# Softmax and MLP on one core: value products in halves, row maxima computed in the MLP, one score bank in four copied by VectorE

## The chip, the core and the metric

The kernel runs on one core of a Trainium2 chip. The metric is the device time of one execution in microseconds (us), median of several runs. PE is TensorE, PEld its weight loads, DVE is VectorE, ACT is ScalarE, POOL is GpSimd, and SP is the engine whose queue issues most of the DMAs. PSUM has eight banks of 128 x 512 f32; scores and products land there.

## What is computed

For x of 2048 tokens by 448 channels:

```
g = sigmoid((x * gate_w).sum(-1, keepdims=True))
# attention, 16 heads of 28 channels, one shared key and value head
q = (x @ wq) per head; k = x @ wk; v = x @ wv
p = softmax(q k^T * 28 ** -0.5)
a = (p v) of all heads @ wo
# token mixer and MLP
h  = gelu(layernorm(x) @ w1);  hs = shifted h @ w2;  x1 = x + hs
b  = x1 + gelu(layernorm(x1) @ w3) @ w4          # 448 -> 1792 -> 448
out = g * a + (1 - g) * b
```

Most products are made in three passes of fp32r, from high and low parts of both operands; the value products and the output projection are plain f32.

## The kernel before

All engines follow the order in which the program text issues their instructions; each engine works through its own queue in order, and semaphores join the queues.

**First stage** (to about 100 us): query projections for 16 units, keys, values and gate go to a DRAM tensor qd and come back in other layouts. A unit u = 4b + g is a block b of 512 tokens with a group g of four heads; its queries are a tile of 128 x 512, 32 rows per head, of which 28 hold queries, and two rows (28 and 29) are free for the negative row maximum in a high and a low part. They multiply two rows of ones in the keys, so the scores come out with the maximum already subtracted.

**MLP** (to about 402 us): for each of four blocks b, 14 iterations f of 128 hidden channels. `w3_part` (L614) makes 11 matmuls into one of two banks, ACT takes gelu twice (gh rounded at L625, gf in f32 at L626), DVE subtracts for the low part gl (L627). The second layer follows two iterations later: `w4_part` (L630), three matmuls for each of four token tiles into four accumulation banks. In the last block the function `fill` (L610) slips in the one maximum that unit 0 needs. A maximum is `max_all` (L200): four matmuls of the query tile with 32 keys per head (khd) and a reduction on DVE, then `max_end` (L220): negate, split, transpose on DVE, and eight small DMAs on SP that write the two rows into the unit's query tile qh. The maximum is taken over 32 keys only; sums that come out too large are found at the end, and then a branch, not taken here, computes everything again.

**Attention** (to about 954 us): 16 units of eight steps v, two key tiles of 128 keys each. `q_begin` (L718) splits the queries of a unit into qh and ql, two units ahead, at v=6. In a step:

- `scores` (L795), for each of the two key tiles: three passes, each of four matmuls (one per head, in four row groups), into four banks taken from the front of a list;
- `exps` (L803): ACT exponentiates the four banks into SBUF tiles p and returns each bank to the end of the list. READ is the order, DRAIN (empty) the banks that DVE would copy first, `late_exps` their exponentials;
- at v=2 the maximum of the next unit (`max_all`, `max_end`) and `recip` of the last unit's sums, at v=3 `norm`;
- at v=4 to 7 `wo_job` (L757): the output projection of the last unit, one token tile, into one bank, and `wo_add` (L774), which DVE adds to the output;
- `values` (L817) of the step before: eight f32 matmuls of 512 columns into one bank, and DVE adds it to the tile o (L828; at the first step a copy, L826).

The list holds all eight banks. With f32 operands each matmul is two records in the trace. `sums_begin` (L735) fetches the sums, `recip` (L740) takes their reciprocals and sends them through DRAM to 128 partitions, `norm` (L751) multiplies. A closing part (L870 on) finishes the last unit's tokens.

Of the kernel before, what the change touches and what calls it, by code (L numbers as in the profile page):

```python
# [16 lines left out]
P = 128  # L17
# [19 lines left out]
def f32(ap):  # L37
    return ap.bitcast(F32)
# [3 lines left out]
def gated_mix_kernel(  # L42
# [44 lines left out]
    def misc_tile(name):  # L87
        return psA.tile([P, 512], F32, tag="misc", bufs=1, name=name)
# [86 lines left out]
    def q_load(u, raw):  # L175
        b, g = divmod(u, NG)
        qr_of[u] = raw
        nc.sync.dma_start(raw, qd[g, :, 512 * b:512 * b + 512])
# [13 lines left out]
    NU = NB * NG  # L192
    qr_of, qh_of, ql_of = {}, {}, {}
    mx_of = {}
    mc_of = {}

    def max_tile(name):
        return psA.tile([P, 512], F32, tag="mx", bufs=1, name=name)
# [1 line left out]
    def max_all(u, ps):  # L200
        mx_of[u] = late.tile([P, 4, 4], F32, tag="mr", bufs=1, name=f"mr_{u}")
        for t in range(4):
            nc.tensor.matmul(ps[:, t * P:(t + 1) * P], qh_of[u][:, t * P:(t + 1) * P], khd, start=True, stop=True)
        nc.vector.reduce_max(mx_of[u].rearrange("p j t -> p t j"), ps.rearrange("p (t j k) -> p t j k", t=4, j=4), axis=AX.X)
# [12 lines left out]
                nc.vector.reduce_max(mr[:, j, t:t + 1], mk, axis=AX.X)  # L217
        mx_of[u] = mr

    def max_end(u):  # L220
        mr = mx_of.pop(u).rearrange("p j t -> p (j t)")
        mc = late.tile([P, 32], F32R, tag="mc", bufs=1, name=f"mc_{u}")
        nc.vector.tensor_scalar(mc[:, 0:16], mr, -1.0, None, op0=ALU.mult)
        nc.vector.scalar_tensor_tensor(mc[:, 16:32], mr, -1.0, f32(mc)[:, 0:16],
                                       op0=ALU.mult, op1=ALU.subtract)
        mrow = late.tile([P, 32], F32, tag="mrow", bufs=1, name=f"mrow_{u}")
        nc.vector.transpose(mrow, f32(mc))
        for k in range(2):
            for p in range(4):
                r = 32 * p + 16 * k  # L230
                nc.sync.dma_start(
                    f32(qh_of[u])[DH + k:P:32, :].rearrange("j (t p q) -> p j t q", p=4, q=32)[p], mrow[r:r + 16, :])

    ctx2 = ExitStack()

# [366 lines left out]
    with tc.tile_pool(name="s2", bufs=1, reuse_waits="tile") as s2, \  # L602
# [2 lines left out]
            for n in range(n0, n1):  # L605
                nc.gpsimd.tensor_scalar(x1[:, n, :], x1[:, n, :], gi[:, n:n + 1], None, op0=ALU.mult)

        fills = [lambda: max_all(0, misc_tile("m_0")), lambda: max_end(0)]

        def fill():  # L610
            if fills:
                fills.pop(0)()

        def w3_part(b, f):  # L614
            i, k = divmod(f, 2)
# [23 lines left out]
        for b in range(NB):  # L639
            acc = [ps2.tile([P, 512], F32, tag="acc", bufs=4, name=f"acc_{b}_{t}") for t in range(4)]  # L640
            gs = {}
            for f in range(NF):
                if f == 9 and b + 1 < NB:
                    mv, rs = layernorm_stats(s2a, b + 1)
                if f == 10 and b + 1 < NB:
                    xt4 = big(f"xt4_{b + 1}")[:, 0:4 * D].rearrange("p (f t j) -> p f t j", f=NE, t=4)
                if f in (10, 11) and b + 1 < NB:
                    for t in (2 * f - 20, 2 * f - 19):
                        xn = s2a.tile([P, 512], F32, tag="xn", bufs=1, name=f"xn_{b + 1}_{t}")[:, 0:D]
                        layernorm_norm(b + 1, t, mv, rs, xn, xt4)  # L650
                if f == 11 and b + 1 < NB:
                    xt_write(b + 1, xt4)
                    ln_read(b + 1)
                gs[f] = w3_part(b, f)
                if b == 0 and f % 2 and f < 11:
                    split_w3((f + 3) // 2)
                    split_w4((f + 3) // 2)
                    if f < 9:
                        load_w34((f + 5) // 2, s2a if f == 1 else s2)
                if b == 1 and f == 0:  # L660
                    nc.gpsimd.tensor_tensor(gg, invE, gz, ALU.pow)
                    nc.vector.tensor_scalar(gg, gg, 1.0, None, op0=ALU.add)
                    nc.vector.reciprocal(gg, gg)
                    nc.vector.tensor_scalar(gi, gg, -1.0, 1.0, op0=ALU.mult, op1=ALU.add)
                if b == NB - 1 and f == 4:
                    weigh_x1(0, 4 * b)
                if b == 1 and f in (0, 2, 4, 6):
                    load_k(f // 2, s2a.tile([P, 512], F32, tag="xn", bufs=1, name=f"kf_{f // 2}"))
                if b == 1 and f in (1, 3, 5, 7):
                    split_k(f // 2)  # L670
                if b == 2 and f == 1:
                    nc.gpsimd.memset(f32(khd), 0.0)
                    for j in range(4):
                        nc.sync.dma_start(f32(khd)[32 * j:32 * j + DH, j, :], f32(kH)[0:DH, 0:MK])
                    q_load(0, s2a.tile([P, 512], F32, tag="xn", bufs=1, name="qr_0"))
                if b == 2 and f == 5:
                    q_split(0, qh0, ql0)
                if f >= 2:
                    for t in range(4):
                        w4_part(f - 2, t, gs[f - 2], acc)  # L680
                        if b > 2 and t % 2 == 0 and f < NF - 1:
                            fill()
            for t in range(4):
                w4_part(NF - 2, t, gs[NF - 2], acc, NF - 2 if b == NB - 1 else NF - 1)
                if b + 1 < NB:
                    ln_split(b + 1, t, t + 1)
# [7 lines left out]
        assert not fills  # L694
    ctx2.close()


    with tc.tile_pool(name="s3", bufs=1, reuse_waits="tile") as s3, \
# [7 lines left out]
        def take():  # L706
            return banks.pop(0)
# [107 lines left out]
                nc.scalar.activation(p_of[u, kt][j], p_of[u, kt][j], AF.Exp, scale=SCALE)  # L815

        def values(u, v, add=True):  # L817
            pv = take()
            for kt in (2 * v, 2 * v + 1):
                ps = p_of.pop((u, kt))  # L820
                for j in range(4):
                    nc.tensor.matmul(pv[32 * j:32 * j + 32, :], vext[:, kt, :], ps[j],  # L822
                                     start=(kt % 2 == 0), stop=(kt % 2 == 1), tile_position=(0, 32 * j))
            if v == 0:
                o_of[u] = s3.tile([P, 512], F32, tag="o", bufs=2, name=f"o_{u}")
                nc.vector.tensor_copy(o_of[u], pv)  # L826
            elif add:
                nc.vector.tensor_add(o_of[u], o_of[u], pv)  # L828
            else:
                return pv  # L830
            banks.append(pv)

        READ = (0, 1, 2, 3)
        DRAIN = ()
        WO_AT = (4, 5, 6, 7)
        M_AT = 2

        for k in range(NU * NV):
            u, v = divmod(k, NV)
            if v == 6 and u + 2 < NU:  # L840
                q_begin(u + 2)
                q_fetch(u + 3)
            for kt in (2 * v, 2 * v + 1):
                exps(u, kt, scores(u, kt))
            for kt in (2 * v, 2 * v + 1):
                late_exps(u, kt)
            if v == 2 and sums:
                norms.append(recip(*sums.pop()))
            if v == 3 and norms:
                norm(*norms.pop())  # L850
            if v == M_AT and u + 1 < NU:
                ps = take()
                max_all(u + 1, ps)
                banks.append(ps)
                max_end(u + 1)
            job = None
            if v in WO_AT:
                if u:
                    job = wo_job(u - 1, WO_AT.index(v))
                else:  # L860
# [10 lines left out]
        pv = values(u, NV - 1, False)  # L871
# [4 lines left out]
        tq = [bank(f"oq_{t}")[:, 0:P] for t in range(4)]  # L876
        rr = s3.tile([P, 2, 2, 4], F32, name="rr4")
        on4 = s3.tile([P, 4, P], F32, name="on4")

# [30 lines left out]

        def keep_warm(n):
            for _ in range(n):
                nc.tensor.matmul(banks[0][:, 0:256], warm[:, 0:P], warm, start=True, stop=True)

        for t in range(4):
            nc.vector.tensor_add(o[:, toks[t]], o[:, toks[t]], pv[:, toks[t]])
# [35 lines left out]
        with tc.If(again > 0, label="redo"):  # L952
            for b in range(NB):
                for g in range(NG):
# [1 line left out]
                    q_fetch(u)  # L956
                    q_begin(u)
                    max_full(u, bank)
                    max_end(u)
# [67 lines left out]
```

## Time and profile before

| what | us |
|---|---|
| median of 3 runs | 971.56 (971.14 to 971.71) |
| the profiled execution | 970.74 |
| its span | 968.9 |
| ACT busy in the span | 647.0 |
| DVE busy in the span | 345.7 |

The profile is one execution. A row of a timeline gives the start and the length in us, the engine, the line, the operation, the tiles written and read, and in brackets the idle time of the engine before it with what ended it. A row of a group gives count, busy time, mean length in ns and idle time before. A row of a table by stretches gives, after the stretch and its length, the busy time of PE, PEld, DVE, ACT and POOL with their instruction counts, the granted share of the TensorE clock, the share of the DMA engines and their GB/s. The end of matmuls is modelled, so a PE that looks busy may be waiting.

### The profile page before, as it was taken

The numbers are of one execution on the slowest core, as the hardware profiler recorded it, in microseconds if no ns is written. First come the engines' busy times: TensorE is split into PE (matmuls) and PEld (weight loads), VectorE is DVE, ScalarE is ACT, GpSimd is POOL, SyncE is SP. The second block draws the span as 40 slices with busy tenths as digits, with TensorE's granted clock in tenths as the row PEclk, the third lists the DMA queues.
The fourth block names the chain that finished last, engine by engine and source line by source line (L and its number), as shares of the span: only waits on it lengthen the run. The fifth ranks groups of instructions, "written<-read, shape, count | busy, mean of one in ns | idle before, by whom it ended". The sixth has DMA issues, their size and how long they took to land. (4 is left out here: it accounts for less than half of the span.)

```text
span 968.9 us, 19222 instructions
## 1 busy us (share of the span) xinstructions
PE 960.1 (99%) x7571; PEld 589.3 (61%) x7571; DVE 345.7 (36%) x636; ACT 647.0 (67%) x1262; POOL 74.9 (8%) x105
## 2 busy tenths in 40 slices
PE   9999999999999999999999999999999999999996
PEld 7788888888888888644444444444444444444442
DVE  5663354433413421233333333333233332333323
ACT  5532444422222222589999999999999999999993
POOL 2242200221002400200000000000000000000000
PEclk9999999999999999999999999999999999999999
DMA  9703342300300300100000010000010000100001
GB/s 317 263 27 76 103 162 83 89 22 10 93 1 1 82 1 1 60 13 14 14 23 14 24 50 24 14 13 24 24 51 15 14 25 13 53 23 2 13 13 42
DMA packets 38753, 46.22 MB, mean 48 GB/s; under 512 B 8880, under 2 KB 27008, under 8 KB 38656
## 3 DMA queue, kind: packets, MB, share of 16 engines
q1 hardware_dynamic: 35632, 39.45, 13.6%
q10 hardware_dynamic: 3024, 5.47, 1.6%
q8 instruction: 61, 1.00, 0.4%
q14 instruction: 36, 0.29, 0.1%
HBM read 32.85 MB, written 11.67 MB: 46 GB/s over the span
## 5 line engine op out<-in xcount | busy, mean ns | idle before, releaser
L810 ACT ACTIVATE p<-bank 128x512 f32<-128x512 f32 x1024 | 510.9, 653 | 42.7 <-PE bank L800 42.7
L822 PE MATMUL bank<-p,vext 128*32 128x512 f32 x2048 | 245.9, 598 | 0.0
L800 PEld LDWEIGHTS bank<-qh,kH 30*128 30x128 f32 x1024 | 86.2, 182 | 141.8 <-ACT p L810 128.4
L800 PE MATMUL bank<-qh,kH 30*128 30x512 f32 x1024 | 168.4, 465 | 0.1
L625 ACT ACTIVATE gh<-g 128x512 fp32r<-128x512 f32 x55 | 32.8, 597 | 187.6 <-PE g L134 187.6
L800 PE MATMUL bank<-qh,kL 28*128 28x512 f32 x1024 | 137.9, 404 | 0.0
L822 PEld LDWEIGHTS bank<-p,vext 128*32 128x32 f32 x2048 | 59.9, 110 | 127.3 <-issue 101.1
L800 PE MATMUL bank<-ql,kH 28*128 28x512 f32 x1024 | 131.3, 389 | 0.0
L828 DVE TENSOR_TENSOR o<-o,bank 128x512 f32<-128x512 f32 x111 | 76.3, 687 | 123.9 <-PE bank L822 72.9
L627 DVE TENSOR_TENSOR gl<-gf,gh 128x512 fp32r<-128x512 f32 x55 | 38.3, 696 | 168.0 <-ACT gf L626 168.0
L636 PE MATMUL acc<-w4l,gh 128*128 128x448 f32 x220 | 80.4, 366 | 0.0
L635 PE MATMUL acc<-w4h,gh 128*128 128x448 f32 x220 | 80.4, 365 | 0.0
L637 PE MATMUL acc<-w4h,gl 128*128 128x448 f32 x220 | 80.3, 365 | 0.0
L800 PEld LDWEIGHTS bank<-ql,kH 28*128 28x128 f32 x1024 | 73.6, 185 | 9.6
L131 PE MATMUL g<-al,w3h 128*128 128x512 f32 x168 | 65.7, 391 | 0.0
L130 PE MATMUL g<-ah,w3h 128*128 128x512 f32 x168 | 65.6, 390 | 0.0
L132 PE MATMUL g<-ah,w3l 128*128 128x512 f32 x168 | 65.6, 390 | 0.0
L800 PEld LDWEIGHTS bank<-qh,kL 28*128 28x128 f32 x1024 | 62.1, 184 | 0.0
L763 PE MATMUL bank<-wof,on 128*32 128x448 f32 x512 | 61.2, 551 | 0.0
L775 DVE SCALAR_TENSOR_TENSOR ot<-bank,gg,ot 128x448 f32<-128x448 f32 x44 | 30.1, 684 | 85.7 <-PE bank L763 56.9
L635 PEld LDWEIGHTS acc<-w4h,gh 128*128 128x128 f32 x220 | 41.3, 188 | 4.7
L902 POOL TENSOR_TENSOR ot<-y,ot 128x448 f32<-128x448 f32 x1 | 1.2, 1162 | 553.5 <-ACT y L901 553.5
(188 smaller groups left out, 997.1 us busy)
## 6 DMA issues: line engine op xcount, KB each, us to landing
qd<-qf ACTq DMA_DIRECT2D x16, 256.0 KB
qr<-qd SPq DMA_DIRECT2D x16, 256.0 KB
rb<-rd SPq DMA_DIRECT2D x15, 256.0 KB
x<-in_x_dram SPq DMA_DIRECT2D x4, 896.0 KB
xd<-xt SPq DMA_DIRECT2D x16, 224.0 KB
w34raw<-in_w_dram SPq DMA_DIRECT2D x7, 512.0 KB
out_dram<-ot SPq DMA_DIRECT2D x15, 224.0 KB
w34raw<-in_w_dram SPq DMA_DIRECT2D x7, 448.0 KB
```

Source lines behind the costliest of these rows:

```text
L130: nc.tensor.matmul(ps, wh[:, c, :], ah[:, c, :], start=(c == 0), stop=False)
L131: nc.tensor.matmul(ps, wh[:, c, :], al[:, c, :], start=False, stop=False)
L132: nc.tensor.matmul(ps, wl[:, c, :], ah[:, c, :], start=False, stop=False)
L627: nc.vector.tensor_sub(gl, gf, f32(gh))
L635: nc.tensor.matmul(ps, gh[:, tok], w4h[i][:, k, :], start=(f == 0), stop=False)
L636: nc.tensor.matmul(ps, gh[:, tok], w4l[i][:, k, :], start=False, stop=False)
L637: nc.tensor.matmul(ps, gl[:, tok], w4h[i][:, k, :], start=False, stop=(f == stop))
L763: nc.tensor.matmul(ps[32 * j:32 * j + 32, 0:D], on_of[u][:, tok], wof[:, g, :], start=True, stop=True, tile_position=(0, 32 * j))
L800: nc.tensor.matmul(bs[j], w, a, start=(i == 0), stop=(i == 2), tile_position=(32 * j, 0))
L810: nc.scalar.activation(ps[j], bs[j], AF.Exp, scale=SCALE)
L822: nc.tensor.matmul(pv[32 * j:32 * j + 32, :], vext[:, kt, :], ps[j], start=(kt % 2 == 0), stop=(kt % 2 == 1), tile_position=(0, 32 * j))
L828: nc.vector.tensor_add(o_of[u], o_of[u], pv)
```

## The change

- **Maxima.** All 16 are computed in the MLP, one per iteration: units 0 to 6 in block 2 at f=2 to 8, units 7 to 15 in block 3 at f=0 to 8. For each, SP loads the unit's queries from qd (`max_load`), DVE rounds them into qh0 (`max_cast`, ahead of the iteration's second-layer matmuls on PE and behind gl on DVE), PE and DVE take the maximum behind the second layer, and in the next iteration the two rows go to qd by eight DMAs, four on SP and four on ACT (`max_send`). In the attention the query loads bring the rows along. `max_end` no longer sends; only the branch at the end still asks it to.
- **Values.** Each step's value products are made in two halves of 256 columns, each with a bank of its own, and DVE adds each half by itself.
- **Banks.** READ is (0, 3, 1, 2) and DRAIN is (3,): DVE copies the fourth head's bank to p in SBUF and returns it; ACT exponentiates that copy in place, behind the six other exponentials of the step.
- **Reciprocals.** `recip` moves from v=2 to the end of v=1, `norm` from v=3 ahead of the values to the end of v=3.
- The load of unit 0's queries moves to block 3, f=11, and its split to f=13; the closing part takes another bank for the matmuls that keep PE's clock up.

```diff
-    def max_end(u):
+    def max_end(u, again=False):
...
         nc.vector.transpose(mrow, f32(mc))
+        row_of[u] = mrow
+        if again:
+            max_send(u, f32(qh_of[u]), nc.sync)
+
+    def max_send(u, q, other):
+        mrow = row_of.pop(u)
         for k in range(2):
             for p in range(4):
                 r = 32 * p + 16 * k
-                nc.sync.dma_start(
-                    f32(qh_of[u])[DH + k:P:32, :].rearrange("j (t p q) -> p j t q", p=4, q=32)[p], mrow[r:r + 16, :])
+                (other if k else nc.sync).dma_start(
+                    q[DH + k:P:32, :].rearrange("j (t p q) -> p j t q", p=4, q=32)[p], mrow[r:r + 16, :])
...
-        fills = [lambda: max_all(0, misc_tile("m_0")), lambda: max_end(0)]
...
+        def max_load(u):
+            if u < NU:
+                q_load(u, s2a.tile([P, 512], F32, tag="xn", bufs=1, name=f"qm_{u}"))
+
+        def max_cast(u):
+            qh_of[u] = qh0
+            nc.vector.tensor_copy(qh0, qr_of.pop(u))
+            max_load(u + 1) if u != 6 else None
...
+                    max_load(0)
+                u = f - 2 if b == 2 and 2 <= f <= 8 else f + 7 if b == 3 and f <= 8 else None
+                if b == 2 and f == 12:
+                    max_load(7)
+                if row_of:
+                    w, = row_of
+                    max_send(w, qd[w % NG, :, w // NG * 512:w // NG * 512 + 512], nc.scalar)
+                if u is not None:
+                    max_cast(u)
+                if b == NB - 1 and f == 11:
                     q_load(0, s2a.tile([P, 512], F32, tag="xn", bufs=1, name="qr_0"))
-                if b == 2 and f == 5:
+                if b == NB - 1 and f == 13:
                     q_split(0, qh0, ql0)
                 if f >= 2:
                     for t in range(4):
                         w4_part(f - 2, t, gs[f - 2], acc)
-                        if b > 2 and t % 2 == 0 and f < NF - 1:
-                            fill()
+                if u is not None:
+                    max_all(u, max_tile(f"m_{u}") if u % 2 else misc_tile(f"m_{u}"))
+                    max_end(u)
...
         def values(u, v, add=True):
-            pv = take()
...
+            pvs = []
+            for q in (slice(0, 256), slice(256, 512)):
+                pv = take()
+                for kt in (2 * v, 2 * v + 1):
+                    for j in range(4):
+                        nc.tensor.matmul(pv[32 * j:32 * j + 32, q], vext[:, kt, :], p_of[u, kt][j][:, q],
+                                         start=(kt % 2 == 0), stop=(kt % 2 == 1), tile_position=(0, 32 * j))
+                if v == 0:
+                    nc.vector.tensor_copy(o_of[u][:, q], pv[:, q])
+                elif add:
+                    nc.vector.tensor_add(o_of[u][:, q], o_of[u][:, q], pv[:, q])
+                pvs.append(pv)
+                if add:
+                    banks.append(pv)
+            return pvs
+
+        READ = (0, 3, 1, 2)
+        DRAIN = (3,)
...
-            if v == 2 and sums:
-                norms.append(recip(*sums.pop()))
-            if v == 3 and norms:
-                norm(*norms.pop())
-            if v == M_AT and u + 1 < NU:
-                ps = take()
-                max_all(u + 1, ps)
-                banks.append(ps)
-                max_end(u + 1)
...
                 values(*divmod(k - 1, NV))
-                if v == 0:
-                    sums.append(sums_begin(u - 1, o_of[u - 1]))
+            if u and v == 0:
+                sums.append(sums_begin(u - 1, o_of[u - 1]))
+            if u and v == 1:
+                norms.append(recip(*sums.pop()))
+            if u and v == 3:
+                norm(*norms.pop())
```

More of the change, by code (lines that the diff above doesn't have):

```diff
@@ L194, in gated_mix_kernel @@
     mx_of = {}
-    mc_of = {}
+    row_of = {}
     def max_tile(name):
@@ L606, in weigh_x1 @@
                 nc.gpsimd.tensor_scalar(x1[:, n, :], x1[:, n, :], gi[:, n:n + 1], None, op0=ALU.mult)
-        fills = [lambda: max_all(0, misc_tile("m_0")), lambda: max_end(0)]
-        def fill():
-            if fills:
-                fills.pop(0)()
+        def max_load(u):
[5 more added lines that the diff above has]
+            max_load(u + 1) if u != 6 else None
         def w3_part(b, f):
@@ L693, in gated_mix_kernel @@
                 nc.vector.tensor_add(xt, xt, acc[t][:, 0:D])
-        assert not fills
     ctx2.close()
@@ L817, in values @@
         def values(u, v, add=True):
-            pv = take()
[L819 to L823, printed above, removed]
             if v == 0:
                 o_of[u] = s3.tile([P, 512], F32, tag="o", bufs=2, name=f"o_{u}")
[L826 to L834, printed above, removed]
+            pvs = []
[15 more added lines that the diff above has]
+        DRAIN = (3,)
         WO_AT = (4, 5, 6, 7)
-        M_AT = 2
         for k in range(NU * NV):
@@ L865, in gated_mix_kernel @@
                 values(*divmod(k - 1, NV))
-                if v == 0:
-                    sums.append(sums_begin(u - 1, o_of[u - 1]))
+            if u and v == 0:
[4 more added lines that the diff above has]
+                norm(*norms.pop())
         assert not sums and not norms
         u = NU - 1
-        pv = values(u, NV - 1, False)
+        pvs = values(u, NV - 1, False)
         o = o_of[u]
@@ L875, in gated_mix_kernel @@
         tp = [bank(f"ot_{i}").rearrange("p (t n) -> p t n", t=4) for i in range(2)]
-        tq = [bank(f"oq_{t}")[:, 0:P] for t in range(4)]
+        tq = [bank(f"oq_{t}") for t in range(4)]
+        spare = tq[3]
+        tq = [ps[:, 0:P] for ps in tq]
         rr = s3.tile([P, 2, 2, 4], F32, name="rr4")
@@ L912, in keep_warm @@
             for _ in range(n):
-                nc.tensor.matmul(banks[0][:, 0:256], warm[:, 0:P], warm, start=True, stop=True)
+                nc.tensor.matmul(spare[:, 0:256], warm[:, 0:P], warm, start=True, stop=True)
         for t in range(4):
-            nc.vector.tensor_add(o[:, toks[t]], o[:, toks[t]], pv[:, toks[t]])
+            nc.vector.tensor_add(o[:, toks[t]], o[:, toks[t]], pvs[t // 2][:, toks[t]])
         with tc.block():
@@ L958, in gated_mix_kernel @@
                     max_full(u, bank)
-                    max_end(u)
+                    max_end(u, True)
                     pv = take()
```

## The prediction

> **What bounds the kernel now.** I read the page, the groups, then the timeline of each engine in three places: one unit of the attention, the MLP around its one maximum, and the seam between them.
>
> ```profile
> PE 960.1 (99%) x7571; PEld 589.3 (61%) x7571; DVE 345.7 (36%) x636; ACT 647.0 (67%) x1262; POOL 74.9 (8%) x105
> ACT  5532444422222222589999999999999999999993
> L810 ACT ACTIVATE p<-bank 128x512 f32<-128x512 f32 x1024 | 510.9, 653 | 42.7 <-PE bank L800 42.7
> L737 SPq DMA_DIRECT2D rt<-o x15: 569/572/582, 442.7 to 923.8; - x15
> ```
>
> PE's 99% is modelled, so it settles nothing. The MLP (slices 5 to 16) leaves ACT mostly idle, the attention fills it: 510.9 us of exponentials, 42.7 us of waiting for scores. The sum of each unit is fetched once a unit, so a unit lasts (923.8 - 442.7) / 14 = 34.36 us. One unit on ACT:
>
> ```profile
> 572.01 4.03 ACT L810 ACTIVATE p<-bank 128x512 f32<-128x512 f32 x8 [0.41 <-PE bank L800]
> 576.46 11.89 ACT L810 ACTIVATE p<-bank 128x512 f32<-128x512 f32 x24 [0.42 <-PE bank L800]
> 588.86 7.95 ACT L810 ACTIVATE p<-bank 128x512 f32<-128x512 f32 x16 [0.51 <-PE bank L800]
> 597.49 4.03 ACT L810 ACTIVATE p<-bank 128x512 f32<-128x512 f32 x8 [0.68 <-PE bank L800]
> 601.91 3.54 ACT L810 ACTIVATE p<-bank 128x512 f32<-128x512 f32 x7 [0.40 <-PE bank L800]
> ```
>
> Eight exponentials take 4.03, the last about 0.65 of it, so one starts every (4.03 - 0.65) / 7 = 0.48, and a step of eight needs 3.84. Steps v=0 to 2 (the third with the maximum) take 12.40 together, v=3 and 4 take 8.63, v=5 takes 4.42, and v=7, in the first row, 4.45. So ACT sets v=0 and 3; the maximum costs v=2 some 0.6; something else sets v=4 to 7, the steps with a projection. PE in v=7, with DVE's add:
>
> ```profile
> 570.96 0.51 PE L800 MATMUL bank<-qh,kH 30*128 30x512 f32 x4
> 571.30 0.41 PE L800 MATMUL bank<-qh,kL 28*128 28x512 f32 x4
> 571.53 0.41 PE L800 MATMUL bank<-ql,kH 28*128 28x512 f32 x4
> 571.76 0.66 PE L800 MATMUL bank<-qh,kH 30*128 30x512 f32 x4
> ...
> 572.26 0.62 PE L800 MATMUL bank<-ql,kH 28*128 28x512 f32 x3
> 572.81 0.96 PE L763 MATMUL bank<-wof,on 128*32 128x448 f32 x8
> 573.59 1.90 PE L822 MATMUL bank<-p,vext 128*32 128x512 f32 x16
> 575.42 0.50 PE L800 MATMUL bank<-qh,kH 30*128 30x512 f32 x4
> ```
> ```profile
> 571.17 0.69 DVE L828 TENSOR_TENSOR o<-o,bank 128x512 f32<-128x512 f32 x1 [0.68 <-ACT p L810]
> ```
>
> This is a loop: scores to first exponential 1.05 (570.96 to 572.01), that to projection 0.80, projection to values 0.78, values to the next scores 1.83: 4.46. In the second key tile the fourth matmul starts at 571.76 + 0.66 - 0.50 = 571.92, 0.06 after the add at L828 freed its bank (571.17 + 0.69). Its later passes trail by one slot, and the projection starts 1.05 after 571.76. Unblocked it would be 0.23 + 0.23 + 0.32 = 0.78 (the last pass's last matmul starts at 572.49, 0.32 before the projection).
>
> **The change, part by part.** *Sixteen maxima in the MLP.* One is there already:
>
> ```profile
> 342.53 0.60 ACT L625 ACTIVATE gh<-g 128x512 fp32r<-128x512 f32 x1 [1.41 <-PE g L134]
> 347.98 0.60 ACT L625 ACTIVATE gh<-g 128x512 fp32r<-128x512 f32 x1 [4.36 <-PE g L134]
> 352.92 0.60 ACT L625 ACTIVATE gh<-g 128x512 fp32r<-128x512 f32 x1 [3.85 <-PE g L134]
> ```
> ```profile
> 343.65 0.69 DVE L627 TENSOR_TENSOR gl<-gf,gh 128x512 fp32r<-128x512 f32 x1 [1.80 <-ACT gf L626]
> 344.26 0.68 DVE L204 TENSOR_REDUCE mr<-m 128x16 f32<-128x512 f32 x1
> ```
> ```profile
> 342.11 0.39 PE L134 MATMUL g<-ah,w3l 128*128 128x512 f32 x1
> 342.33 0.36 PE L635 MATMUL acc<-w4h,gh 128*128 128x448 f32 x1
> ```
> ```profile
> L183 DVE CAST qh<-qr 128x512 fp32r<-128x512 f32 x16 | 6.7, 420 | 5.1 <-DMA qr<-qd 5.1
> ```
>
> The iteration with it lasts 5.45, the next 4.94: 0.51 each, 15 new ones 7.65. Each also waits for a new cast of the queries into qh0, which stands on DVE behind gl. With G the start of gh: gl starts at G + 1.12, the next DVE work 0.61 later, the cast (0.42) ends at G + 2.15. From f=2 on PE has 12 second-layer matmuls first, from G - 0.20 (342.33): 4.94 less eleven first-layer passes of 0.22 leaves about 0.2 each, so the maximum's weights could load during the twelfth, at G + 2.0. That is 0.15 of waiting, 14 times, 2.1 (bounds 0 and 4). At b=3, f=0 and 1 nothing stands between: the weights could load during the last first-layer pass, at G - 0.42 (342.11), and wait until G + 2.2, so 2.6 twice, 5.2. Queued behind that wait is all of the next first-layer tile. Eight row sends, four on SP and four on ACT, and a query load per iteration stand beside ACT's 1.1 us and DVE's 2.5 us of work in 4.94: nothing. The attention loses 0.6 in v=2 and its row sends.
>
> *One bank of four through DVE.* DVE copies score bank 3 to SBUF; ACT exponentiates it after the other six of the step.
>
> ```profile
> L826 DVE COPY o<-bank 128x512 f32<-128x512 f32 x16 | 11.1, 691 | 55.1 <-ACT p L810 49.2 <-PE bank L822 3.2 <-DMA qr<-qd 2.7
> L574 ACT CAST ah<-xr 128x512 fp32r<-128x512 f32 x16 | 8.7, 620 | 1.6 <-DMA xr<-xd 1.6
> L290 ACT COPY qf<-q 128x512 f32<-128x512 f32 x16 | 9.4, 587 | 26.4 <-PE q L134 18.4 <-DMA qd<-qf 5.6 <-PE q L302 1.5
> L112 DVE TENSOR_TENSOR w3l<-w34raw,w3h 128x256 fp32r<-128x256 f32 x21 | 7.7, 419 | 0.1
> ```
>
> ACT still does all eight. From SBUF (L574) it took 620 ns, from PSUM (L290) 587; I add 0.04 to two of eight, so the floor rises to 3.93 (bounds 3.84 and 3.95). [...] In return banks come back without ACT: v=1 falls from about 4.05 to 3.93, and v=4, whose second tile now waits for exponentials 6 to 8 of v=3, from 8.63 - 3.84 = 4.79 to the pace of the others. DVE gains two copies, 1.38, and two half adds in place of one, 0.15 more; with the projection's add it is busy 2.9 of 4.4, in time for each release by my count (margins of 0.1 us; if they go, 0.1 a step).
>
> *Values in halves.* The second half's add is 0.42 (L112), not 0.69, and ends before the second tile's scores: the 0.06 block goes. What is late next is the first exponential's bank, which the projection takes: 0.60 plus 0.06 in place of 0.80. Sixteen weight loads become 32 with half the columns behind each. Values cost nothing more if eight passes keep the pace of four; at 0.23 a pass, as the score passes go, 8 x 0.23 = 1.84 comes before the drain and the loop grows by about 0.1. I take 0.06, between them. Loop: 1.05 + 0.66 + 0.78 + 1.89 = 4.38 (bounds 4.20, PE's own work alone: 0.80 + 0.78 + 0.78 + 1.84, and 4.46).
>
> *Reciprocals further apart.*
>
> ```profile
> 446.88 0.25 DVE L744 RECIPROCAL rr<-rt 128x16 f32<-128x16 f32 x1
> 453.71 0.69 DVE L753 TENSOR_TENSOR on<-o,rb 128x512 f32<-128x512 f32 x1 [2.32 <-DMA rb<-rd]
> ```
>
> The product waits for its DMA, 6.8 after the reciprocal. In the new places they are two steps apart, 7.9: covered by 1 us, else DVE's copies queue behind.
>
> *The seam.*
>
> ```profile
> 402.67 6.76 SPq L178 DMA_DIRECT2D qr<-qd  x2
> 403.14 7.94 ACT L810 ACTIVATE p<-bank 128x512 f32<-128x512 f32 x16 [3.37 <-PE bank L800]
> 407.91 0.43 DVE L183 CAST qh<-qr 128x512 fp32r<-128x512 f32 x1 [5.05 <-DMA qr<-qd]
> 408.38 0.69 DVE L184 TENSOR_TENSOR ql<-qr,qh 128x512 fp32r<-128x512 f32 x1
> 412.59 0.60 ACT L810 ACTIVATE p<-bank 128x512 f32<-128x512 f32 x1 [1.51 <-PE bank L800]
> ```
> ```profile
> 406.00:408.00 2.00, 2.00 (x13) 0.85 (x11) 0.09 (x1) 2.00 (x6) 0.69 (x1) 0.94 0.56 212
> 408.00:410.00 2.00, 2.00 (x12) 0.40 (x12) 1.03 (x2) 2.00 (x6) 0.00 (x0) 0.50 0.00 0
> ```
>
> DVE waits 5 us for unit 1's queries. The first copies stand behind that: the first ends near 409.7, so ACT idles from 406.0 and PE stands from 404.2. Two steps took 9.45 (to 412.59); now the second step starts at 410.9 and the third at 414.8 with a full clock, near 416 with the half clock of 408 to 410: 2.2 to 3.5 more, 3.3 taken.
>
> *Clock.* The trace halves PE's clock near 408 though matmuls ran from 404 to 408. The gaps at f=0 and 1 are shorter, 2.4 each. I charge one halved spell of 3.4 us, 1.7 (bounds 0 and 3.4). [...]
>
> **Sum.** MLP 7.65 + 2.1 + 5.2 + 1.7 = +16.6. Seam +3.3; rest of unit 0 -1.0. Each of units 1 to 14: 0.09 x 2 (v=0, 3) - 0.12 - 0.59 (v=2: 12.40 - 3.84 - 4.05 = 4.51) - 0.41 - 3 x 0.06 = -1.1, -15.4. Unit 15 and the end 0. Total +3.5 on the profiled 970.74, or on the median of 971.56, 0.8 above it: **975**, own range 971 to 979. The measurement tells 0.2%, 2 us, from no change.
>
> **The rivals.** *Faster: the projection steps fall to PE's own work.* If the projection does not wait for the first exponential but starts when PE is through, the loop is 4.20: 0.18 x 4 x 15 = 10.8 less, **964**. It decides below 4.32, where the sum turns negative. For it: today the projection starts 0.14 after that bank can be free, so PE's order binds. Against: with the block gone that release is next. *The change does not do what it says:* the halves leave the loop at 4.46: 0.08 x 60 = 4.8 more, 980. *Copies late:* a wait on DVE (reciprocal, product) holds the banks of the next step once a unit, about 1 us: 16 more, **991**; against it 1 us of cover.
>
> **How the numbers follow.** Forecast 0.42, faster loop 0.33, no gain in the loop 0.15, late copies 0.10. Range 963 to 983: it leaves out the late copies and the ends. Faster 0.33, same 0.14, slower 0.53: the fast case, a tenth of the forecast on either edge of the bound, the rest.
>
> **What would show it.** Iterations of the MLP with a maximum near 5.6; two gaps of 2.4 on PE at the start of b=3, waiting for the new cast; ACT without gaps in v=0 to 3 at 3.93 a step and with gaps of 0.4 in v=4 to 7; the third step of unit 0 some 13 after the first. It is wrong if projection steps run under 4.3, or if DVE waits for a DMA inside a unit.

## The result and the profile after

| | before | after |
|---|---|---|
| median of 5 runs each, us | 971.14 (970.50 to 971.71) | 976.36 (975.08 to 977.31) |
| span of the profiled execution | 968.9 | 974.2 |

The ratio is 1.0052, interval 1.0038 to 1.0067: the changed kernel is slower by half a per cent. To see where, cut the span at three events that both traces have: the first gelu of the MLP, the first exponential, the end of the last exponential. These are ACT's rows of the kernel after (in brackets, the idle time before the row and what ended it), and below them those of the kernel before (its first exponential, at 403.14, stands in the prediction):

```profile
133.12 0.60 ACT L634 ACTIVATE gh<-g 128x512 fp32r<-128x512 f32 x1 [3.67 <-PE g L134]
423.07 3.04 ACT L829 ACTIVATE p<-bank 128x512 f32<-128x512 f32 x6 [3.37 <-PE bank L819]
956.80 1.19 ACT L834 ACTIVATE p<-p 128x512 f32<-128x512 f32 x2
```
```profile
130.11 0.60 ACT L625 ACTIVATE gh<-g 128x512 fp32r<-128x512 f32 x1 [3.42 <-PE g L134]
951.75 1.63 ACT L810 ACTIVATE p<-bank 128x512 f32<-128x512 f32 x3
```

| stretch, us | before | after | difference |
|---|---|---|---|
| start to first gelu (code not touched) | 130.11 | 133.12 | +3.0 |
| MLP, to the first exponential | 273.03 | 289.95 | +16.9 |
| attention, to the end of the last exponential (953.38, 957.99) | 550.24 | 534.92 | -15.3 |
| closing part, to the end of the span | 15.5 | 16.2 | +0.7 |

So the change moves a lot and little is left of it. **The MLP.** An iteration with a maximum, start of gh to start of gh, and all matmuls of the maxima as one group:

```profile
287.47 0.60 ACT L634 ACTIVATE gh<-g 128x512 fp32r<-128x512 f32 x1 [4.37 <-DMA qd<-mrow]
292.99 0.60 ACT L634 ACTIVATE gh<-g 128x512 fp32r<-128x512 f32 x1 [4.43 <-PE g L134]
```
```profile
L203 PE MATMUL m<-khd,qh 128*128 128x128 f32 x64 | 10.1, 281 | 4.7 <-DVE qh L620 4.7
```

The iteration takes 5.52 in place of 4.94, and all 64 matmuls of the maxima together wait 4.7 for the cast. PE's rows at the start of the last block show where they wait. The table below them, by stretches of 3.4 us, shows what follows (the two spells in which the clock was halved lasted 3.41 each, from 348.00 to 351.41 and from 354.83 to 358.24):

```profile
346.98 0.63 PE L203 MATMUL m<-khd,qh 128*128 128x128 f32 x4 [2.38 <-DVE qh L620]
...
349.62 0.63 PE L130 MATMUL g<-ah,w3h 128*128 128x512 f32 x1
...
354.10 0.63 PE L203 MATMUL m<-khd,qh 128*128 128x128 f32 x4 [2.33 <-DVE qh L620]
```
```profile
344.60:348.00 3.40, 1.02 (x7) 0.97 (x8) 1.43 (x3) 1.08 (x2) 1.95 (x2) 1.00 0.02 5
348.00:351.40 3.40, 3.40 (x10) 2.56 (x8) 0.90 (x4) 0.00 (x0) 0.00 (x0) 0.50 0.26 73
351.40:354.80 3.40, 1.07 (x7) 0.73 (x6) 1.06 (x3) 1.09 (x2) 0.00 (x0) 1.00 0.02 3
354.80:358.20 3.40, 3.40 (x9) 2.65 (x9) 1.23 (x4) 0.00 (x0) 0.00 (x0) 0.50 0.28 78
```

The third number from the right is the granted clock, 1.00 or 0.50: after both stretches in which PE worked for about 1.0 us of 3.4 (1.02 and 1.07), the next ran at half clock. The iterations f=0 and 1 take 7.17 and 7.13 us in place of 2.49.

**The seam** from the MLP to the attention. SP, DVE, ACT and PE at the start of unit 0 in the kernel after:

```profile
422.61 6.66 SPq L178 DMA_DIRECT2D qr<-qd  x2
...
427.76 0.43 DVE L183 CAST qh<-qr 128x512 fp32r<-128x512 f32 x1 [4.96 <-DMA qr<-qd]
428.22 0.69 DVE L184 TENSOR_TENSOR ql<-qr,qh 128x512 fp32r<-128x512 f32 x1
428.83 1.28 DVE L827 COPY p<-bank 128x512 f32<-128x512 f32 x2
429.55 1.23 ACT L834 ACTIVATE p<-p 128x512 f32<-128x512 f32 x2 [3.43 <-DVE p L827]
...
429.57 0.80 PE L819 MATMUL bank<-qh,kH 30*128 30x512 f32 x3 [5.35 <-DVE p L827]
```

DVE waits 4.96 for unit 1's queries, the two copies stand behind that, and PE waits 5.35 for the banks. The third step of unit 0 starts 12.64 after the first (7.78 and 4.86), in place of 9.45.

**One unit later on.** ACT's rows (line 829 from the banks, line 834 from the copies), and PE's in the step at 613.91:

```profile
597.66 3.08 ACT L829 ACTIVATE p<-bank 128x512 f32<-128x512 f32 x6
600.52 1.25 ACT L834 ACTIVATE p<-p 128x512 f32<-128x512 f32 x2
601.57 3.13 ACT L829 ACTIVATE p<-bank 128x512 f32<-128x512 f32 x6
...
613.91 3.05 ACT L829 ACTIVATE p<-bank 128x512 f32<-128x512 f32 x6 [0.25 <-PE bank L819]
...
618.25 3.05 ACT L829 ACTIVATE p<-bank 128x512 f32<-128x512 f32 x6 [0.26 <-PE bank L819]
```
```profile
614.57 0.96 PE L782 MATMUL bank<-wof,on 128*32 128x448 f32 x8
615.34 1.91 PE L844 MATMUL bank<-p,vext 128*32 128x256 f32 x32
617.18 0.51 PE L819 MATMUL bank<-qh,kH 30*128 30x512 f32 x4
```

A step without a projection takes 601.57 - 597.66 = 3.91 without a gap on ACT. One with a projection takes 4.34 here: first exponential to projection 0.66, projection to values 0.77, values to scores 1.84, scores to first exponential 1.07. ACT's gap in it is 0.25, where it was 0.41. Mean starts of units 1 to 14, in us by step:

| | v=0 | 1 | 2 | 3 | 4 | 5 | 6 | 7 | unit |
|---|---|---|---|---|---|---|---|---|---|
| before | 3.83 | 4.05 | 4.52 | 3.83 | 4.81 | 4.42 | 4.43 | 4.45 | 34.34 |
| after | 3.92 | 3.91 | 3.91 | 3.91 | 4.53 | 4.33 | 4.31 | 4.32 | 33.14 |

### The profile page after: what moved, and what is told of

The parts are those of the page before. It is cut to its first block, busy times and chain, and to the rows that moved or that the text cites. A ratio compares the mean times of both kernels' runs of the same rounds, so it can differ in the third digit from the quotient of the medians.

```text
span 974.2 us, 23521 instructions
## 1 busy us (share of the span) xinstructions
PE 925.7 (95%) x9619; PEld 638.2 (66%) x9619; DVE 542.5 (56%) x1035; ACT 651.0 (67%) x1262; POOL 74.8 (8%) x105
## 5 line engine op out<-in xcount | busy, mean ns | idle before, releaser
L829 ACT ACTIVATE p<-bank 128x512 f32<-128x512 f32 x768 | 397.0, 678 | 20.1 <-PE bank L819 20.0
L844 PE MATMUL bank<-p,vext 128*32 128x256 f32 x4096 | 246.9, 381 | 20.1 <-ACT p L829 19.5
L844 PEld LDWEIGHTS bank<-p,vext 128*32 128x32 f32 x4096 | 126.3, 110 | 145.3 <-ACT p L829 47.5
L827 DVE COPY p<-bank 128x512 f32<-128x512 f32 x256 | 175.4, 691 | 48.2 <-PE bank L819 47.2
L834 ACT ACTIVATE p<-p 128x512 f32<-128x512 f32 x256 | 161.3, 740 | 3.4 <-DVE p L827 3.4
L849 DVE TENSOR_TENSOR o<-o,bank 128x256 f32<-128x256 f32 x222 | 93.6, 421 | 89.1 <-PE bank L844 82.1
L819 PE MATMUL bank<-qh,kH 30*128 30x512 f32 x1024 | 119.1, 445 | 5.3 <-DVE p L827 5.3
L819 PE MATMUL bank<-qh,kL 28*128 28x512 f32 x1024 | 106.2, 393 | 0.0
L819 PE MATMUL bank<-ql,kH 28*128 28x512 f32 x1024 | 105.9, 390 | 0.0
L819 PEld LDWEIGHTS bank<-qh,kH 30*128 30x128 f32 x1024 | 57.6, 183 | 62.7 <-ACT p L829 51.8
```

The costliest lines, as they stand in the source:

```text
L819: nc.tensor.matmul(bs[j], w, a, start=(i == 0), stop=(i == 2), tile_position=(32 * j, 0))
L827: nc.vector.tensor_copy(ps[j], bs[j])
L829: nc.scalar.activation(ps[j], bs[j], AF.Exp, scale=SCALE)
L844: nc.tensor.matmul(pv[32 * j:32 * j + 32, q], vext[:, kt, :], p_of[u, kt][j][:, q], start=(kt % 2 == 0), stop=(kt % 2 == 1), tile_position ...
L849: nc.vector.tensor_add(o_of[u][:, q], o_of[u][:, q], pv[:, q])
```

## The experiments

The theory: the MLP pays for the maxima, worst where PE has nothing between the first layer and the maximum, and again by the clock; the seam pays because DVE's copies queue behind a split that waits for a load; the attention gains from the maxima's departure, the copies and the halves. Rivals: the waits would only move; the seam is a matter of the clock or of the copies themselves; one part of the change brings the whole gain. All kernels start from the changed one unless said otherwise.

### Maxima of the last block two iterations later

```diff
-... else f + 7 if b == 3 and f <= 8 else None
+... else f + 5 if b == 3 and 2 <= f <= 10 else None
```

> The changed kernel with the nine maxima of the last MLP block two iterations later (f = 2 to 10 in place of 0 to 8). Theory: at f = 0 and 1 there is no down-projection between the up-projection and the maximum, so the tensor engine stands still for the cast (2.38 and 2.33 us) and then runs at half clock; two of the 15 iterations grew by 4.65 us and not by 0.57. Then f = 0 and 1 fall back to 2.49 us each, every iteration with a maximum takes 5.5, and the time falls by 2 x 4.08 = 8.2, to 968.2. Rival: the wait is for the query's load or for the vector engine's backlog of the block's end, and moves along with the first two maxima: f = 2 and 3 then show gaps of 2 us or more and the time stays within 2 us of 976.4.

Measured: 966.98 (964.59 to 968.13), ratio to the kernel before 0.9958 (0.9944 to 0.9971). ACT's rows at the start of the last block:

```profile
344.64 0.60 ACT L634 ACTIVATE gh<-g 128x512 fp32r<-128x512 f32 x1 [5.47 <-PE g L134]
347.13 0.60 ACT L634 ACTIVATE gh<-g 128x512 fp32r<-128x512 f32 x1 [1.41 <-PE g L134]
349.63 0.60 ACT L634 ACTIVATE gh<-g 128x512 fp32r<-128x512 f32 x1 [1.41 <-PE g L134]
355.14 0.60 ACT L634 ACTIVATE gh<-g 128x512 fp32r<-128x512 f32 x1 [4.43 <-PE g L134]
```

f=0 and 1 take 2.49 each, f=2, now with a maximum, 5.51. The MLP takes 281.79, 8.16 less. The rival falls: nothing moved along. The half clock went with the pauses.

### Unit 1's query split four steps later

```diff
         q_fetch(1)
-        q_begin(1)
-        q_fetch(2)
...
+            if k == 4:
+                q_begin(1)
+                q_fetch(2)
```

> The changed kernel with unit 1's query split (a cast and a subtraction on the vector engine, and the next query's load) issued at the fifth step of unit 0 in place of ahead of its first. Theory: the copies of the first two steps stand behind this split in the vector engine's queue, and the split waits for a load; the first two steps took 12.64 us in place of 9.45. Without it they take 9.0 to 9.5 and the half-clock stretch at 426 to 433 us goes or shrinks; the time falls by 3.2, to 973.2. Rival: the step is long because both engines start the loop empty and the copy itself (0.69 us against an exponential of 0.48) delays the late exponentials, or because the clock was halved by the pause ahead of it: the two steps stay over 12 us and the time stays within 0.8 of 976.4.

Measured: 971.09 (969.08 to 972.73), ratio 1.0004 (0.9995 to 1.0013). ACT at the start of unit 0:

```profile
420.83 3.04 ACT L827 ACTIVATE p<-bank 128x512 f32<-128x512 f32 x6 [3.37 <-PE bank L817]
423.71 1.19 ACT L832 ACTIVATE p<-p 128x512 f32<-128x512 f32 x2
424.76 3.08 ACT L827 ACTIVATE p<-bank 128x512 f32<-128x512 f32 x6
427.62 1.25 ACT L832 ACTIVATE p<-p 128x512 f32<-128x512 f32 x2
428.66 3.13 ACT L827 ACTIVATE p<-bank 128x512 f32<-128x512 f32 x6
```

The first two steps take 7.83, less than I expected and less than the 9.45 of the kernel before: with 3.93 and 3.90 neither is stretched by a half clock in this execution. Unit 0 falls from 38.11 to 33.39. The half clock is not gone for good: of the five kernels with a later split, four of them below, three had one there, and their second step took 4.84 to 5.02. The cause is the order on DVE; the copies themselves delay nothing.

### Without the copies, without the halves, without both

```diff
-        READ = (0, 3, 1, 2)
-        DRAIN = (3,)
+        READ = (0, 1, 2, 3)
+        DRAIN = ()
```

> The changed kernel without the vector engine's copies: all four score banks are read by their exponentials, as in the kernel before; the moved maxima and the halves stay. Theory (halves shorten the loop in the steps with a projection, copies only help where a bank is late): steps 6 to 8 of a unit stay at 4.32, the fifth goes back to about 4.8, the second to 4.0, and the others fall by 0.08, net +0.2 a unit or +3; the seam's first two steps come back from 12.64 to 9.5, -3.2; total within 1.5 of 976.4. Rival (the copies shorten the loop, since a bank that the vector engine empties does not wait its turn in the scalar engine's queue): steps 6 to 8 go back to 4.45 as well, +0.57 a unit or +8.5, less 3.2 at the seam: 981 to 982.

```diff
-            for q in (slice(0, 256), slice(256, 512)):
+            for q in (slice(0, 512),):
```

> The changed kernel with the values whole again (one bank, 512 columns, one vector-engine addition a step); the copies and the moved maxima stay. Theory (halves shorten the loop): steps 6 to 8 of a unit go back from 4.32 to 4.45, the fifth from 4.53 to 4.65, the four without a projection stay at 3.91, where the scalar engine sets them: +0.5 a unit, +7.5, 984. Rival (the copies shorten it, the halves do nothing): all steps stay within 0.03 and the time within 1 of 976.4. Second rival (the halves cost, because 16 more matmuls and a bank more are taken in each step): steps 6 to 8 fall to 4.25 or less, 973 or less.

The third kernel has both diffs:

> The changed kernel with neither the copies nor the halves: what is left of the change is the maxima in the MLP and the order of reciprocals. It is the fourth corner of a square: copies and halves 33.14 us a unit, copies alone 33.30, halves alone 33.76, the kernel before 34.34. Theory (the maximum's own bank and reduction in each unit cost about half of what was gained, the copies the rest, halves alone nothing): 33.65 a unit, third step 3.9 in place of 4.52, steps 6 to 8 at 4.44, first four 3.85 to 4.05; the seam's first two steps 9.5; total 976.4 + 15 x 0.5 - 3.2 = 980.8. Rival (the copies alone bring the gain; a maximum in the attention was hidden): 34.2 to 34.3 a unit, 990.

| | us | v=0 | 1 | 2 | 3 | 4 | 5 | 6 | 7 | unit |
|---|---|---|---|---|---|---|---|---|---|---|
| changed | 976.36 | 3.92 | 3.91 | 3.91 | 3.91 | 4.53 | 4.33 | 4.31 | 4.32 | 33.14 |
| no copies | 980.86 | 3.93 | 3.97 | 3.94 | 3.97 | 4.68 | 4.42 | 4.43 | 4.42 | 33.76 |
| no halves | 974.01 | 3.92 | 3.90 | 3.90 | 3.90 | 4.53 | 4.36 | 4.41 | 4.38 | 33.30 |
| neither | 979.27 | 3.84 | 4.05 | 3.93 | 3.96 | 4.67 | 4.43 | 4.44 | 4.43 | 33.75 |

ACT in two projection steps of the kernel without copies (compare the 0.25 above):

```profile
611.96 4.03 ACT L829 ACTIVATE p<-bank 128x512 f32<-128x512 f32 x8 [0.66 <-PE bank L819]
616.38 4.03 ACT L829 ACTIVATE p<-bank 128x512 f32<-128x512 f32 x8 [0.39 <-PE bank L819]
```

My theory of the halves falls here. Without the copies the halves bring nothing (33.76 against 33.75); with them 0.16 a unit. The copies bring 0.45 a unit alone and 0.62 with the halves, and the maxima's departure the other 0.59 (34.34 to 33.75, together with the reciprocals' new order, which no run has by itself). In the loop of v=6 and 7 one term tells the four kernels apart: from the first exponential to the projection it takes 0.78 with neither, 0.75 with the halves alone, 0.71 with the copies alone and 0.65 with both, and the other terms agree within 0.03. The "no halves" time is below that of the changed kernel, but in the execution that has a profile not by its steps in the attention: it entered the MLP at 130.19 and not 133.12, and its iteration f=0 of the last block took 5.57 and not 7.17. That second point is a test by itself. PE's row and the stretches of that kernel:

```profile
344.09 0.63 PE L203 MATMUL m<-khd,qh 128*128 128x128 f32 x4 [2.37 <-DVE qh L620]
```
```profile
342.96:346.38 3.42, 2.29 (x12) 2.02 (x13) 2.25 (x6) 0.00 (x0) 0.71 (x1) 1.00 0.27 74
346.38:349.79 3.41, 1.08 (x7) 0.61 (x5) 1.03 (x2) 1.08 (x2) 0.00 (x0) 1.00 0.03 6
349.79:353.20 3.41, 3.41 (x11) 2.83 (x11) 1.25 (x4) 0.00 (x0) 0.00 (x0) 0.50 0.29 78
```

The same pause of 2.37, from 341.72 to 344.09, lay across the border of two stretches at 342.96, counted back from the half clock at 349.79 in lengths of 3.41 (the clock's changes in the changed kernel, at 348.00, 351.41, 354.83, 358.24, 426.51 and 433.33, lie 1, 1, 1, 20 and 2 such lengths apart): the one that holds 1.13 of it still has 2.29 of work, the one ahead 2.17, and neither is followed by a half clock. The pause of f=1 lay within one stretch, and the next is halved. So, by these two iterations, a pause with its maximum costs 5.57 - 2.49 = 3.08, and the half clock behind it another 7.14 - 5.57 = 1.57.

### The pauses filled with matmuls

```diff
+                if b == 3 and f < 2:
...
+                    for _ in range(9):
+                        nc.tensor.matmul(ps, w3h[0][:, 0, 0:P], acts[b][0][:, 0, :], start=True, stop=True)
```

> The changed kernel with nine matmuls of 128 by 512 that are used for nothing, put ahead of the maximum in the first two iterations of the last MLP block, where the tensor engine stood still for 2.38 and 2.33 us (they write the maximum's bank, which the maximum then overwrites). Theory (the pause itself halves the clock for the next window): the tensor engine works through the pause, the clock stays at full, and the two iterations take 2.49 + 2.4 + 0.6 = 5.5 each in place of 7.15, -3.3 in all. Rival (the clock is halved for another reason, or the cast comes later too, since the filler delays nothing but the maximum): the iterations stay at 7.1, or grow to 9 if the filler stands behind a wait of its own.

One run: 972.24. PE's rows of the two maxima, and the stretch behind the first of them, with the clock third from the right:

```profile
346.93 0.66 PE L203 MATMUL m<-khd,qh 128*128 128x128 f32 x4 [0.79 <-DVE qh L620]
352.40 0.66 PE L203 MATMUL m<-khd,qh 128*128 128x128 f32 x4 [0.20 <-DVE qh L620]
```
```profile
347.50:351.00 3.50, 3.50 (x17) 2.90 (x17) 1.25 (x4) 0.80 (x2) 0.00 (x0) 1.00 0.29 76
```

The iterations take 6.05 and 5.46 in place of 7.17 and 7.13, 2.8 less, and the clock stays at 1.00: with work in the pause no half clock followed. The first came 0.6 over the expectation.

### Both mends

> Both mends at once: the maxima of the last block two iterations later, and unit 1's query split at the fifth step of unit 0. Theory: the two costs lie in stretches that do not touch, so they add: -8.2 in the MLP, -4.7 in unit 0 (33.4 in place of 38.1), 963.5, faster than the kernel before by 7. Rival: a pause at the seam takes the place of the one removed, or the clock's half-speed window moves elsewhere: 967 or more.

Measured: 962.62 (961.78 to 964.29), ratio 0.9908 (0.9893 to 0.9922). The costs add. Unit 0 took 34.41, one of its steps 5.02 at half clock.

### The first stage: both kernels once more

> The kernel before, once more, for its first stage: its profiled execution began the MLP at 130.1 us, that of the changed kernel at 133.1 with the same code ahead of it. Theory (the moment at which the first weights land and at which the clock is raised varies from one execution to the next): somewhere from 130 to 133.5. Rival (the change does it): 130.1 again.

> The changed kernel once more, unchanged, for its first stage. In the ten profiles so far the MLP began at 130.0 to 133.1 us with the same code ahead of it, at 130.0 and 130.1 in the two of the kernel before. Theory (the first weights land earlier or later from one execution to the next, and the clock is raised at one or another of its steps): anywhere in that range, and the last MLP block's two long iterations may miss the half clock as in the run with whole values. Rival (it belongs to the build): 133.1 again and both iterations at 7.1.

The kernel before took 971.78 and began the MLP at 130.03, the changed one 976.40 and 132.97. By these two both rivals stand. A kernel further down, with the unit's query split and maximum at the third step, has the MLP of the kernel before, and it begins late all the same, so the maxima in the MLP are not the cause. Its stretch from 7 to 10 us, and PE's first row that waits for the weights, then the same stretch of the kernel before:

```profile
7.00:10.00 3.00, 3.00 (x5) 1.20 (x4) 2.73 (x5) 2.49 (x5) 0.00 (x0) 1.00 1.05 382
```
```profile
5.36 1.22 PE L298 MATMUL q<-xkv,wqraw 128*128 128x512 f32 x1 [0.73 <-DMA wqraw<-in_wq_dram]
```
```profile
7.00:10.00 3.00, 3.00 (x12) 1.98 (x11) 1.97 (x5) 1.85 (x4) 0.00 (x0) 1.00 1.04 393
```

Five matmuls in the stretch in place of twelve, and its MLP began at 132.72. In all 14 profiles: where the first query matmul started by 4.67 us, the MLP began at 130.03 to 130.19 (5 of 14); where it waited until 5.31 to 5.51, at 130.72 to 133.12 (9 of 14). Both kinds are seen with the MLP of either kernel. The traces' record of the clock begins, at full speed, at 3.84 to 5.04 us in eight profiles and at 9.04 to 10.15 in six, and those six are all late ones, with the MLP from 132.54 on; ahead of its first entry the tables show 1.00 as well, so no run shows the clock being raised there, as the theory had it. That one and the same kernel can be early and late is not shown: both profiles of the kernel before are early, both of the changed one late, so that it belongs to one build or another is not ruled out. Why the weights land later was not found.

### The maxima back in the attention

The kernel before with the copies, the halves, the reciprocals' order and the late query split; unit 1's maximum at v=6 of unit 0.

```diff
-            if v == M_AT and u + 1 < NU:
+            if v == (2 if u else 6) and u + 1 < NU:
```

> The kernel with both mends and the copies, the halves and the order of reciprocals kept, but the maxima back in the attention (unit u + 1's in the third step of unit u, unit 1's in the seventh step of unit 0; their loads, fills and row transfers as in the kernel before). It prices the move of the maxima by itself: 15 x 0.57 = 8.6 in the MLP against what a maximum costs in the attention. Theory (break even): the MLP falls by 8.6, the third step of a unit goes from 3.91 to about 4.5 and the second to 4.05, +0.6 a unit, +8.9: 962 to 964, against 962.6 with the maxima moved. Rival (with the fourth bank emptied by the vector engine a maximum fits in the slack of a step that the scalar engine sets): the third step stays under 4.1, 956 to 958. Second rival (the reduction now stands between the copies in the vector engine's queue): the third step over 4.8, 967 or more.

Measured: 957.14 (956.26 to 958.54), ratio 0.9863 (0.9847 to 0.9880). ACT over four steps of a unit, v=1 to v=4, with the maximum in the second of them (v=2, from 580.93), and the first row of v=5:

```profile
577.02 3.08 ACT L808 ACTIVATE p<-bank 128x512 f32<-128x512 f32 x6
...
580.93 3.13 ACT L808 ACTIVATE p<-bank 128x512 f32<-128x512 f32 x6
...
585.18 3.05 ACT L808 ACTIVATE p<-bank 128x512 f32<-128x512 f32 x6
...
589.11 3.08 ACT L808 ACTIVATE p<-bank 128x512 f32<-128x512 f32 x6
...
593.46 3.05 ACT L808 ACTIVATE p<-bank 128x512 f32<-128x512 f32 x6 [0.24 <-PE bank L798]
```

The step with the maximum takes 4.25, between theory and rival, and v=4 falls from 4.53 to 4.36: 33.36 a unit, +0.2 against the maxima moved. The MLP takes 273.03 again. So a maximum that cost 0.59 a unit in the attention before (with the reciprocals' order) costs 0.2 there once DVE empties a bank, against 0.57 in the MLP.

### Unit 1's split and maximum at the third step, with halves and without

```diff
-            if k == 4:
+            if k == 2:
...
-            if v == (2 if u else 6) and u + 1 < NU:
+            if v == 2 and u + 1 < NU:
```

> The kernel with the maxima back in the attention, with unit 1's query split at the third step of unit 0 in place of the fifth and its maximum there too, as in every other unit. In the run before, unit 1's maximum at the seventh step made that step 5.01 and the next 5.30 in place of 4.32 each. Theory (the maximum costs little only where the scalar engine sets the step): unit 0's last two steps fall back to 4.39, its third takes 4.3; 957.1 - 1.3 = 955.8. Rival (the split and the wait for its load now stand ahead of the third step's copies): the third step takes 5.5 or more and the time stays at 957 or above.

Measured: 955.66 (954.69 to 955.99), ratio 0.9830 (0.9816 to 0.9843), the fastest of all. Unit 0 takes 33.55 with steps of 3.92, 3.90, 4.26; its last two are 4.39 and 4.38. As the theory had it.

> The same kernel with the values whole again, so that of the whole change only the copies of one score bank and the order of reciprocals are left, with the query split moved. Theory (the copies bring the gain, the halves a little through the bank they free earlier): steps 6 to 8 go from 4.32 to 4.38 each, the others stay, +0.15 a unit, +2.2 against the kernel with halves. Rival (with a maximum in each unit the halves cost a bank that is missing): the third step falls under 4.2 and the time is the same or lower.

Measured: 957.30 (956.90 to 958.25), ratio 0.9852 (0.9837 to 0.9867); v=5 to 7 take 4.37, 4.40 and 4.37, 33.49 a unit against 33.32. The theory holds: the halves are worth 0.17 a unit here. This kernel has of the whole change only the copies and the reciprocals' order, with the later split, and is 14.7 us faster than the kernel before (972.03 here), of the 16.4 that the fastest gains.

## Why the prediction came out right, and where it did not

The time and the sign were right, and the loss was where it was put. Step by step, in the profiled execution:

- **Maxima, 0.51 and 0.15 of waiting each.** 13 of the 15 new ones took 0.57: the wait for the cast from f=2 on did not come (the group's whole 4.7 are the two pauses), only 0.06 beyond the matmuls. 7.6 in place of 8.6.
- **Two pauses at b=3, 2.6 each.** 2.38 and 2.33, in the place named; the later maxima show their cause.
- **One half-clock spell, 1.7.** The term that was too small: two came, 1.57 each by the run without halves. Its length is that of the spell in the kernel before, 3.41 (407.75 to 411.16, at 0.50); how many would come was its author's estimate. The row that it rests on says less than it was taken for: from 404.34 to 407.75 the kernel before has 22 matmuls where the next stretch at full clock, from 411.16, has 40, so PE was partly waiting there, though its modelled row looks busy. With the pauses the two iterations cost 9.3, where these steps and their maxima had 7.9. The MLP's sum, +16.9 against +16.6, is right because two errors cancel.
- **Seam +3.3.** +3.2; the order on DVE is shown as its cause. The half clock is in both sides of this difference (407.75 to 411.16 before, 426.51 to 433.33 after), and it is not the same in every execution: in the second profiles the two steps took 10.89 before and 14.21 after (9.45 and 12.64 in the first).
- **Rest of unit 0, -1.0.** 25.47 in place of 26.57, -1.1.
- **Units 1 to 14, -1.1 each.** -1.20. v=0 and 3 (+0.09, +0.08), v=1 (-0.14) and v=2 (-0.61) are as worked out; v=4 gave 0.28 and not 0.41 (from its first exponential to the projection 0.86, against 0.65 in v=5 to 7; with a maximum at v=2 it is 0.69, and why was not looked into); v=5 to 7 gave 0.09 to 0.13 and not 0.06.
- **Loop, 1.05 + 0.66 + 0.78 + 1.89.** It reads 1.07 + 0.66 + 0.77 + 1.84: the term for the values in halves was 0.05 too long, 32 matmuls of 256 columns took what 16 of 512 had taken (1.84 and 1.83). The loop's 4.32 is just where the faster rival was said to decide; it did not reach 4.20. ACT's gaps are 0.25 and not the 0.4 given as a sign.
- **Values in halves: "the 0.06 block goes".** This reason failed. Halves alone leave the loop at 4.42; the 0.65 from the first exponential to the projection comes only with the copies and the halves together. The copies, which I counted as harmless to the loop, carry the larger part.
- **Floor of ScalarE, 3.93.** 3.91, without a gap. The 0.04 for each exponential from SBUF was its author's estimate: the 33 ns between its rows of 620 and 587, twice, would have made 3.84 into 3.91.
- **Late copies.** No wait inside a unit that matters: the product found its DMA done in all but one of 15 cases, as its own view of the kernel after shows.

```profile
L772 DVE TENSOR_TENSOR on<-o,rb x15: 684/685/693, 476.1 to 940.0; 128x512 f32<-128x512 f32 x15
its engine sat idle before it (us, times) until:
DMA rb<-rd: 0.3, 1
```

- **Unit 15 and the end, 0.** -0.6 and +0.7.
- **Chances.** A tenth of 0.42 on either edge is 0.08 and not the 0.14 given for no change; nothing else rests on it.

These steps give +16.9 + 3.2 - 1.1 - 16.8 - 0.6 + 0.7 = +2.3 against a predicted +3.5. The other 3.0 of the span's 5.3 lie in the first stage, whose code is the same in both kernels. The prediction put nothing there; whether the changed kernel always pays them is open, as said above. That 976.36 lies so near 975 is in part luck: without them it would have been about 973.

## What to carry to other kernels

Price a moved operation in both places, and in the place that it leaves price it again after the rest of the change: a maximum cost 0.59 a unit before, 0.2 once the copies were in, and 0.57 in the MLP, where PE has no slack (an iteration grew from 4.94 to 5.52). A short wait on PE can be paid twice, once more by a half clock (3.08 and then 1.57 here), so put work of its own between a producer on another engine and its use. Where a queue is worked through in order, as DVE's at the seam (two copies stood behind a wait of 4.96), anything that waits for a load goes behind what others need, not ahead of it: that alone was worth 3.7 to 4.7 us here (unit 0 at 34.41 or 33.39 in place of 38.11).

## What the hardware showed that was not expected

- A half clock followed stretches that were not idle: PE worked 1.02, 1.07 and 1.08 us of about 3.4 ahead of three half-clock spells, and with 2.29 of 3.42 ahead, or with the pause filled (3.50 of 3.50), the clock stayed. No threshold can be read from the busy time alone: at the seam a half clock also followed 1.51 us of 3.41 (second profile of the changed kernel, from 422.73) and 1.74 (without halves, from 418.05), and in the kernel before a stretch in which PE's modelled row looks busy throughout (3.41 of 3.41, from 404.34). One and the same pause (2.38 in the changed kernel, 2.37 without halves) was followed by a half clock in one execution and not in the other.
- The first stage differs by up to 3 us between profiles (130.03 to 133.12), with the time at which the first query matmul finds its weights (4.5 to 5.5 us) and the one at which the clock's record begins (3.84 to 10.15): five matmuls from 7 to 10 us in place of twelve.
- ACT takes six exponentials from PSUM and two from SBUF in 3.91 us, where eight from PSUM took 3.83: 0.04 us more for each from SBUF.
